# A fused mLSTM and expert layer on one core: the first chunk's exponents summed by TensorE, three steps moved from VectorE to ScalarE, and a new written order

## The chip, the cores and the metric

One core of a Trainium2 chip runs the whole program. The time of a run is the device time in microseconds (us) from start to end of the program; the span in a profile is the time from its first to its last instruction, and is a little shorter. The engines are TensorE (PE, matrix products into the accumulators in PSUM; PEld is its weight load), VectorE (DVE), ScalarE (ACT), GpSimd (POOL, which cannot read PSUM) and SyncE (SP, which issues the transfers).

## The reference

The first half is a recurrence with gates over 768 steps, for 4 batches and 8 heads of 40 numbers; the second half is an expert layer on its 3072 output rows.

```python
for t in range(S):
    m_new = maximum(f[t] + m, i[t])
    C = exp(f[t] + m - m_new) * C + exp(i[t] - m_new) * outer(v[t], k[t])
    n = exp(f[t] + m - m_new) * n + exp(i[t] - m_new) * k[t]
    y[t] = sigmoid(og[t]) * (C @ q[t]) / maximum(abs(n . q[t]), 1)
    m = m_new
h = x @ w_in                       # 320 -> 1024, x are the rows of y
solu = h * softmax(h)
out = (solu - mean) / sqrt(var + 1e-6) * g_ln @ w_out      # 1024 -> 320
```

The weights come as 64-bit floats, all else as 32-bit floats.

## The kernel before, in words

The sequence is cut into 6 chunks of 128 steps. A chunk of one batch is a unit; the 24 units run chunk by chunk, so units 0 to 3 are the first chunk of the four batches. In a unit the recurrence is done by matrix products: scores (`score`, L1186, keys by queries), times the decay matrix `d` (`p`, L1199), times the values (`intra`, L1253). From the second chunk on, the state `C` carried in is added (`inter`, L1226). All but the last chunk's units make a new state: `upd` (L1342) multiplies the weighted keys `kt` by the values into the one PSUM bank of the ring `so_`, and `add_c` brings it into `C` (L1369 adds; in the first chunk L1371 only copies, by VectorE, two copies of 64x164 a unit).

The decay matrix is exp(G[t] + b[s]) below the diagonal: G is the running sum of the log decays within a chunk (one row per head), and b = i - G - m is one number per step s and head. In chunks 1 to 5 a transfer spreads the rows of G over the partitions (`gb`), GpSimd masks it (L1102), and ScalarE takes the exponential with b as a bias per partition. Since a bias belongs to one head, this takes 8 ACTIVATEs of 128x128 a unit (`decay`, L1142). In the first chunk no transfer is used: `broad` (L1128) spreads G by 8 products a unit, each with one column of the identity as weights, into a PSUM tile of the ring `ph` (two tiles of 128x1024); the 8 exponentials read it there, and GpSimd masks the result.

A row of the unit's output is then divided (`rd`, L1269 and L1270; `sy` or `x`, L1274), gated (`x`), scaled by its largest number (`xm`, `xr`) and split into two 16-bit halves (`xq`, L1381 by ScalarE and L1388 by VectorE), turned by a transfer (`xT`), and multiplied with w_in (L1437, 16 products of 128x512 into `ph`, which is 128x1024). Row maximum (L1453), exponential (L1467), product (L1485), squares (L1495), a second split (`us`, L1546 and L1550), a second turning transfer into `big`, and 24 products with w_out (L1598) into `so_` follow.

Beside the first units the weights are prepared. `decode` turns a piece of 64-bit numbers into 32-bit ones: ScalarE scales the high words (`wt`, L677); for w_in it also scales the low words (`ls`, L686), and VectorE joins both (L694) and sets the sign (L738). For w_out (4 pieces of 128x640) VectorE shifts the high words (L711), brings in the low words itself (L727) and sets the sign (L738). w_in needs a scale known only when all six loads have landed (L793 to L849). w_out is later multiplied with a gain and a mean (L984), and split (L1000, L1008).

The order is written out by hand: `ORDER` is a list of operation numbers, of which a row may be a pair (two groups of products taken in turn) or may hold a number of keep-warm products to issue first (`fill`; L478, identity by identity, result unused). Each engine issues its own instructions in that order and waits in front of the first that isn't ready; so do the transfers on SP's queue.

## Time and profile before

| | |
|---|---|
| three runs | 298.85, 301.63 and 302.25 us, median 301.63 |
| the profiled execution | 300.66 us, of which 298.9 us are the span |
| busy in the span | PE 288.3 us, DVE 234.5, ACT 192.9, POOL 184.5 |
| mean granted TensorE clock | 0.989 of full speed |
| transfers | 56.13 MB, of which 35.69 MB are read from HBM |

A busy PE is not PE at its peak, since products are pipelined and their ends modelled. So the number that counts for PE here is the distance between the starts of two products, and whether another engine's instruction ended the wait before one.

### The profile page before, as it was taken

The numbers are of one execution on the slowest core, as the hardware profiler recorded it, in microseconds if no ns is written. First come the engines' busy times: TensorE is split into PE (matmuls) and PEld (weight loads), VectorE is DVE, ScalarE is ACT, GpSimd is POOL, SyncE is SP. The second block draws the span as 40 slices with busy tenths as digits, with TensorE's granted clock in tenths as the row PEclk, the third lists the DMA queues.
The fourth block names the chain that finished last, engine by engine and source line by source line (L and its number), as shares of the span: only waits on it lengthen the run. The fifth ranks groups of instructions, "written<-read, shape, count | busy, mean of one in ns | idle before, by whom it ended". The sixth has DMA issues, their size and how long they took to land.

```text
span 298.9 us, 6516 instructions
## 1 busy us (share of the span) xinstructions
PE 288.3 (96%) x2274; PEld 228.5 (76%) x2274; DVE 234.5 (78%) x605; ACT 192.9 (65%) x421; POOL 184.5 (62%) x241
## 2 busy tenths in 40 slices
PE   6789999989999999999999999999999999999995
PEld 6679997776588788786888888887787777756673
DVE  5788999977998887888878878977779878786221
ACT  2569569664587667858766857656766759565343
POOL 7047376960957795648963858649747453875321
PEclk9999999977999999999999999999999999999999
DMA  6979999375576685999969999788886981563811
GB/s 215 282 204 311 346 236 269 120 157 138 151 171 148 150 217 155 272 179 241 228 162 185 203 250 281 177 201 157 254 187 143 258 150 46 128 161 81 206 47 44
DMA packets 82640, 56.13 MB, mean 188 GB/s; under 512 B 66992, under 2 KB 73328, under 8 KB 82608
## 3 DMA queue, kind: packets, MB, share of 16 engines
q1 hardware_dynamic: 82608, 55.72, 76.4%
q8 instruction: 18, 0.29, 0.4%
q14 instruction: 14, 0.11, 0.1%
HBM read 35.69 MB, written 4.03 MB: 133 GB/s over the span
## 4 chain that ended last, share of the span: by engine, by line
PE 72%; DVE 15%; ACT 4%; DMA 3%; issue 3%; SPq 1%; POOL 0%; POOLq 0%; ACTq 0%; DVEq 0%
PE ph L1437 26%; PE sy L1253 8%; PE sy L1186 5%; PE sy L1226 4%; DMA big<-in_w_in_dram 3%; DVE p L1199 2%; DVE xq L1388 1%; DVE wg L738 1%; PE so__2413 L1598 1%; DVE wg L984 1%; PE so__999 L1598 1%; PE so__1676 L1598 1%; PE so__2597 L1598 1%; PE so__3057 L1598 1%; PE so__1227 L1598 1%
## 5 line engine op out<-in xcount | busy, mean ns | idle before, releaser
L1437 PE MATMUL ph<-wih,xT 128*128 128x512 f16 x240 | 76.1, 385 | 0.0
L1598 PEld LDWEIGHTS <-big 128*128 128x128 f16 x576 | 60.7, 110 | 19.6 <-issue 0.8
L1253 PEld LDWEIGHTS sy<-tk,p 128*128 128x128 f32 x384 | 59.8, 198 | 5.7 <-DVE sy L1239 1.1
L1437 PEld LDWEIGHTS <-xT 128*128 128x128 f16 x384 | 46.1, 122 | 21.7 <-issue 2.2
L1142 ACT ACTIVATE d<-gb,bG 128x128 f32<-128x128 f32 x160 | 49.9, 390 | 19.6 <-POOL gb L1102 7.1
L1253 PE MATMUL sy<-tk,p 128*128 128x41 f32 x384 | 57.8, 253 | 0.7 <-DVE sy L1239 0.7
L1550 POOL TENSOR_TENSOR us<-e,us 128x1024 f16<-128x1024 f32 x23 | 49.0, 2130 | 9.6 <-ACT us L1546 9.4
L1437 PE MATMUL ph<-wil,xT 128*128 128x512 f16 x144 | 49.2, 387 | 0.0
L1467 ACT ACTIVATE e<-ph,nh,hs 128x1024 f32<-128x1024 f32 x24 | 28.8, 1198 | 21.0 <-DVE nh L1460 15.5
L1453 DVE TENSOR_REDUCE nm<-ph 128x1 f32<-128x1024 f32 x24 | 29.2, 1216 | 7.7 <-PE ph L1437 7.6
L1199 DVE TENSOR_TENSOR p<-sy,d 128x512 f32<-128x512 f32 x48 | 32.3, 681 | 2.4 <-PE sy L1186 2.2
L1485 DVE SCALAR_TENSOR_TENSOR e<-ph,s,e 128x1024 f32<-128x1024 f32 x24 | 30.7, 1277 | 2.5 <-ACT e L1467 2.0
L1226 PEld LDWEIGHTS sy<-C,qk 128*128 128x128 f32 x160 | 26.9, 191 | 3.2 <-PE ph L1437 0.7
L1495 ACT ACTIVATE sq<-e,a 128x1024 bf16<-128x1024 f32 x24 | 27.4, 1140 | 2.1 <-DVE e L1485 2.1
L1546 ACT CAST us<-e 128x1024 f16<-128x1024 f32 x23 | 23.8, 1036 | 7.3 <-DVE e L1485 7.3
L1186 PE MATMUL sy<-qk 40*128 40x128 f32 x384 | 27.9, 285 | 0.0
L1580 POOL TENSOR_TENSOR pw<-ab,mhalf 128x1 f32<-128x1 f32 x24 | 14.2, 592 | 21.4 <-DVE ab L1574 21.2
L1186 PEld LDWEIGHTS sy<-qk 40*128 40x128 f32 x384 | 23.3, 187 | 4.0 <-issue 2.5
L1226 PE MATMUL sy<-C,qk 128*128 128x82 f32 x160 | 26.0, 258 | 0.2 <-DVE p L1199 0.2
L1304 POOL TENSOR_TENSOR x<-x,sg 128x320 f32<-128x320 f32 x20 | 17.3, 865 | 14.2 <-DVE x L1274 13.9
L1102 POOL TENSOR_SCALAR_AFFINE_SELECT gb<-gb 128x1024 f32<-128x1024 f32 x20 | 22.5, 1125 | 5.1 <-DMA gb<-gd 4.9
L1168 POOL TENSOR_TENSOR kt<-tk,d 128x320 f32<-128x320 f32 x20 | 16.4, 820 | 12.2 <-PE so__3024 L1342 3.2
(257 smaller groups left out, 572.7 us busy)
## 6 DMA issues: line engine op xcount, KB each, us to landing
gb<-gd SPq DMA_DIRECT2D x20, 512.0 KB
tk<-in_tok_dram SPq DMA_DIRECT2D x24, 324.0 KB
qk<-in_qkT_dram SPq DMA_DIRECT2D x48, 160.0 KB
sg<-in_og_dram SPq DMA_DIRECT2D x12, 320.0 KB
out_dram<-ot SPq DMA_DIRECT2D x24, 160.0 KB
big<-in_w_out_dram SPq DMA_DIRECT2D x4, 640.0 KB
big<-in_w_in_dram SPq DMA_DIRECT2D x4, 512.0 KB
big<-in_w_in_dram SPq DMA_DIRECT2D x2, 256.0 KB
```

The source lines that it names most:

```text
L1142: nc.scalar.activation(out=P[d_t][:, j, n, :], in_=exponent(P, h), func=AF.Exp, bias=P[BG][:, 0, c, b * H + h : b * H + h + 1],)
L1186: nc.tensor.matmul(P[ps[j]][:, n * L : (n + 1) * L], lhsT=P[qk][r, 1, n, :], rhs=P[qk][r, 0, n, :], start=True, stop=True,)
L1199: lambda P, j=j: V.tensor_tensor(out=P[p_t][:, j], in0=P[ps[j]].rearrange("p (n l) -> p n l", l=L), in1=P[d_t][:, j], op=ALU.mult,),
L1226: nc.tensor.matmul(P[yk][:, n * 2 * E1 : (n + 1) * 2 * E1], lhsT=P[qk][:, 0, n, :], rhs=P[old][:, n, :], start=first_of_bank(), stop=False ...
L1253: nc.tensor.matmul(yv(P)[:, h, :], lhsT=P[p_t][:, j, n, :], rhs=v1(P)[:, h, :], start=first_of_bank(), stop=True, skip_group_check=True,)
L1437: nc.tensor.matmul(P[ph][:, j * 512 : (j + 1) * 512], lhsT=P[xT][:, a, :], rhs=P[w][:, k, j * 512 : (j + 1) * 512], start=n == 0, stop=n == 7,
L1453: lambda P: V.tensor_reduce(out=P[nm], in_=P[ph], axis=AX.X, op=ALU.max, negate=True),
L1467: lambda P: nc.scalar.activation(out=P[e], in_=P[ph], func=AF.Exp, bias=P[nh], scale=P[hs], accum_out=P[z]),
L1485: lambda P: V.scalar_tensor_tensor(out=P[e], in0=P[ph], scalar=P[s2], in1=P[e], op0=ALU.mult, op1=ALU.mult, accum_out=P[a]),
L1495: lambda P: nc.scalar.activation(out=P[sq], in_=P[e], func=AF.Square, bias=P[a], scale=-float(DFF), accum_out=P[su]),
L1550: lambda P: nc.gpsimd.tensor_tensor(out=P[us][:, 1], in0=P[e], in1=P[us][:, 0], op=ALU.subtract),
L1598: nc.tensor.matmul(P[po][:, 0:DM], lhsT=uTv(P, a)[:, k, :], rhs=P[w][:, k, :], start=n == 0, stop=n == 23)
```

## The change

1. In the first chunk `broad` issues a second product per head: the weights are b (laid out in a second 128 columns of the tile `e`, the rest of which is zero), the moving operand is one column of the identity, repeated. It adds b[s] to G[t] in PSUM. The exponent is then whole, and `decay` is one ACTIVATE of 128x512 for each of the two halves of a unit, in place of four of 128x128. b for these units is made by two subtractions of 32x128 on VectorE (`mk_b0`), and GpSimd sets the columns to zero first.
2. The state copies of the first chunk go to ScalarE (`nc.scalar.copy`).
3. `W_OUT_ACT` is True: the low words of w_out are scaled by ScalarE, as those of w_in were, and VectorE joins the words in one instruction in place of two.
4. Keep-warm products may also be issued after the first-layer tiles are in use, into the PSUM tile that the next group of products will overwrite.
5. `ORDER` is new. It holds 17 keep-warm products where there were 55; one more stands outside it in both.

```diff
 RANK = {
+    "act cn": (0.76, 0.0, 0.0),
...
 ORDER = [
-    8, 3, 6, 146, 5, 0, 30, 28, 1, 32, 11, 34, 4, 27, 36, 9, 25, 38, 286, 26, 24, (18, -1, 5), 10, 7, 127, 47, 2, 192,
+    8, 5, 11, 6, 12, 7, 32, 34, 0, 36, 38, 1, 4, 9, 26, 40, 3, 2, 29, 129, 288, 27, (20, -1, 3), 10, 49, 128, 13, 130,
...
+            late = self.first[self.fill[2][1]] in issued
+            for _ in range(0 if late else filled.get(n, 0)):
                 self.fill[1](self)
...
+            for _ in range(filled.get(n, 0) if late else 0):
+                self.fill[3](self, self.tiles[new[0]])
...
+    B0 = (*G_, 1)
+    P.op(POOL, 210, lambda P: nc.gpsimd.memset(P[G_][:, S : S + L], 0.0), [B0], prio=-84, lock=False)
...
+    def mk_b0(P):
+        o = P[G_][0 : B * H, S : S + L]
+        V.tensor_tensor(out=o, in0=gt(P, I_)[:, 0:L], in1=gt(P, G_)[:, 0:L], op=ALU.subtract)
+        V.tensor_tensor(out=o, in0=o, in1=gt(P, M_)[:, 0:L], op=ALU.subtract)
...
-    W_IN_ACT, W_OUT_ACT = True, False
+    W_IN_ACT, W_OUT_ACT = True, True
...
                         rhs=P[G_][:, 0:L],
                         start=True,
+                        stop=False,
+                    )
+                    nc.tensor.matmul(
+                        exponent(P, h),
+                        lhsT=P[G_][:, S : S + L],
+                        rhs=P[I][:, r : r + 1].to_broadcast([L, L]),
+                        start=False,
                         stop=True,
                     )
...
         def decay(P, j):
             begun_in.add((*d_t, j))
+            if c == 0:
+                nc.scalar.activation(
+                    out=P[d_t][:, j],
+                    in_=P[src].rearrange("p (i two l) -> p two i l", two=2, l=L)[:, j],
+                    func=AF.Exp,
+                )
+                return
...
-                    V.tensor_copy(out=P[cn][r, :, w], in_=o)
+                    nc.scalar.copy(out=P[cn][r, :, w], in_=o)
```

Three places of the new order follow. The first is TensorE while the first units' decay is made, from the last product of the w_in scale (L837, in the change L855) on. Before, units 0 and 1 have had their spreading products by then, and the list goes on so (`so__267` is unit 0's new state, `qk_112` and `qk_103` hold the queries and keys of units 0 and 1):

```order
L837 MATMUL so__215<-wa_219,ones 128x1
L1186 MATMUL sy<-qk_112 128x128 x8
L478 MATMUL so__215<-ident 128x128
L1342 MATMUL so__267<-tk,kt_97 128x82 x4
L1253 MATMUL sy<-tk,p 128x41 x4
L1128 MATMUL ph<-e,ident 128x128 x8
L1253 MATMUL sy<-tk,p 128x41 x4
L1186 MATMUL sy<-qk_103 128x128 x8
```

In the change (of 32 exponent products of units 1 and 2, which stand in turn, the first two are shown, and of unit 3's 16 none):

```order
L1218 MATMUL sy<-qk_99 128x128 x8
L855 MATMUL so__201<-wa_215,ones 128x1
L1146 MATMUL ph<-e,ident 128x128
L1153 MATMUL ph<-ident,e 128x128
...
L1285 MATMUL sy<-tk,p 128x41 x8
L1218 MATMUL sy<-qk_115 128x128 x8
...
L1374 MATMUL so__450<-tk,kt_108 128x82 x4
L486 MATMUL ph<-ident 128x128 x3
```

Unit 0's products with the values (L1253, now L1285) and its state product (L1342, now L1374) now stand behind the exponents of units 1 and 2, and the state product behind those of unit 3 too.

The second place is VectorE, where unit 0's second 16-bit half has been made (before, the first row here; in the change it stands seven rows ahead) and w_out's pieces are decoded among the first units. Before:

```order
L1388 SCALAR_TENSOR_TENSOR xq<-x,xr,xq 128x64
L711 TENSOR_SCALAR wg<-wt 128x640 x2
L738 SCALAR_TENSOR_TENSOR wf<-big,wf 128x512
L727 SCALAR_TENSOR_TENSOR wg<-big,wg 128x640 x2
L738 SCALAR_TENSOR_TENSOR wg<-big,wg 128x640
L1313 TENSOR_REDUCE xm<-x 128x1
L1314 TENSOR_SCALAR xm<-xm 128x1
L1315 RECIPROCAL xr<-xm 128x1
L1371 COPY C_262<-so__466 64x4x41
```

In the change:

```order
L1231 TENSOR_TENSOR p<-sy,d 128x512 x2
L712 SCALAR_TENSOR_TENSOR wg<-wt,ls 128x640
L756 SCALAR_TENSOR_TENSOR wg<-big,wg 128x640
L1301 RECIPROCAL rd<-sy 128x8
L1302 SCALAR_TENSOR_TENSOR rd<-rd 128x8
L1345 TENSOR_REDUCE xm<-x 128x1
```

The shift and the separate low-word step are one instruction now (L712), and the state copies are gone from this engine.

The third place is ScalarE in the same stretch. Before:

```order
L1142 ACTIVATE d<-ph,bG 128x128 x8
L1381 ACTIVATE xq<-x,xr 128x320
L1142 ACTIVATE d<-ph,bG 128x128 x4
L677 ACTIVATE wt<-big 128x640 x2
L1090 ACTIVATE sg<-sg 128x640
L1142 ACTIVATE d<-gb,bG 128x128 x4
```

In the change (`C_320` and `C_403` are the new states of units 0 and 1):

```order
L1166 ACTIVATE d<-ph 128x512 x3
L887 CAST wih<-wf 128x512
L695 ACTIVATE wt<-big 128x640
L704 ACTIVATE ls<-big 128x640
L1403 COPY C_320<-so__450 64x4x41
L1166 ACTIVATE d<-ph 128x512
L704 ACTIVATE ls<-big 128x640
L1174 ACTIVATE d<-gb,bG 128x128 x4
L1403 COPY C_320<-so__450 64x4x41
L695 ACTIVATE wt<-big 128x640
L704 ACTIVATE ls<-big 128x640
L1403 COPY C_403<-so__528 64x4x41
```

The state copies and the low words stand among the exponentials; the second copy of a state stands behind exponentials of unit 4 (`d<-gb`).

On SP's queue the first write of G to the scratch in HBM (`gd`, L563, now L581), which waits for the running sum, stood ahead of the first loads of tokens (`tk`) and gates (`sg`); now three loads of each stand ahead of it.

More of the change, by code (lines that the diff above doesn't have):

```diff
@@ L384, in run @@
         skip = set(joint.values())
+        self.needs()
+        issued = set()
         for n in order:
@@ L390, in run @@
                 out = out + ops[joint[n]][3]
-            for _ in range(filled.get(n, 0)):
+            late = self.first[self.fill[2][1]] in issued
+            for _ in range(0 if late else filled.get(n, 0)):
                 self.fill[1](self)
-            for k in out:
-                if k[:2] not in self.tiles:
-                    self.tiles[k[:2]] = self.tags[k[0]][1]()
+            new = [k[:2] for k in out if k[:2] not in self.tiles]
+            for k in new:
+                self.tiles[k] = self.tags[k[0]][1]()
+            for _ in range(filled.get(n, 0) if late else 0):
+                self.fill[3](self, self.tiles[new[0]])
+            issued.update((n, joint.get(n, n)))
             if n in joint:
@@ L559, in mlstm_moe_kernel @@
     )
+    def mk_b0(P):
+        o = P[G_][0 : B * H, S : S + L]
+        V.tensor_tensor(out=o, in0=gt(P, I_)[:, 0:L], in1=gt(P, G_)[:, 0:L], op=ALU.subtract)
+        V.tensor_tensor(out=o, in0=o, in1=gt(P, M_)[:, 0:L], op=ALU.subtract)
+    P.op(DVE, 440, mk_b0, [B0], [I_, G_, M_], prio=g0, lock=True)
     for b in range(B):
@@ L1132, in broad @@
                         start=True,
+                        stop=False,
[5 more added lines that the diff above has]
+                        start=False,
                         stop=True,
                     )
-            op(PE, 1900, broad, [src], [I, G_], name="g")
+            op(PE, 3700, broad, [src], [I, G_, B0], name="g")
         def decay(P, j):
             begun_in.add((*d_t, j))
+            if c == 0:
[5 more added lines that the diff above has]
+                return
             for n in range(NP):
@@ L1149, in unit @@
         for j in range(2):
-            op(ACT, 1560, lambda P, j=j: decay(P, j), [(*d_t, j)], [src, (*BG, 0)])
+            op(ACT, 660 if c == 0 else 1560, lambda P, j=j: decay(P, j), [(*d_t, j)], [src] if c == 0 else [src, (*BG, 0)])
         if c == 0:
@@ L1370, in add_c @@
                 else:
-                    V.tensor_copy(out=P[cn][r, :, w], in_=o)
+                    nc.scalar.copy(out=P[cn][r, :, w], in_=o)
             for j in range(2):
-                op(DVE, 322, lambda P, j=j: add_c(P, j), [(*cn, j)], [pu], name="cn")
+                op(DVE if c > 0 else ACT, 322 if c > 0 else 360, lambda P, j=j: add_c(P, j), [(*cn, j)], [pu], name="cn")
             Ccur[b] = cn
@@ L1632, in mlstm_moe_kernel, with idle_in @@
         unit(u)
-    P.fill = (216, idle, (("so_", "idle"), ("ph", "wm")))
+    def idle_in(P, t):
+        nc.tensor.matmul(t[:, 0:L], lhsT=P[I], rhs=P[I], start=True, stop=True)
+    P.fill = (216, idle, (("so_", "idle"), ("ph", "wm")), idle_in)
     with tc.manual_schedule():
```

120 rows, old and new, of the table ORDER are left out of this document.

## The prediction

> **What bounds the kernel now.** I read the page's busy shares and its chain first, then a table of windows cut where the chain changes engine, then the chain in order of time. From the page (busy us of each engine; the chain that ended last, by engine):
>
> ```profile
> PE 288.3 (96%) x2274; PEld 228.5 (76%) x2274; DVE 234.5 (78%) x605; ACT 192.9 (65%) x421; POOL 184.5 (62%) x241
> PE 72%; DVE 15%; ACT 4%; DMA 3%; issue 3%; SPq 1%; POOL 0%; POOLq 0%; ACTq 0%; DVEq 0%
> ```
>
> PE leads, but 15% of the chain is VectorE's. The windows (busy us and instructions of PE, PEld, DVE, ACT and POOL, then clock, transfer share and GB/s) say where:
>
> ```profile
> 0.00:18.00 18.00, 12.98 (x99) 11.69 (x101) 11.07 (x22) 6.21 (x16) 7.46 (x23) 1.00 0.87 249
> 18.00:28.00 10.00, 9.79 (x95) 9.18 (x92) 9.04 (x24) 9.82 (x23) 5.77 (x5) 1.00 0.74 254
> 28.00:38.00 10.00, 10.00 (x103) 9.66 (x101) 9.87 (x18) 6.50 (x17) 4.41 (x4) 1.00 0.95 326
> 38.00:48.00 10.00, 10.00 (x92) 9.43 (x92) 9.80 (x22) 7.11 (x19) 6.47 (x5) 1.00 1.00 264
> 48.00:63.40 15.40, 13.74 (x102) 10.69 (x100) 14.95 (x39) 10.57 (x25) 11.88 (x14) 1.00 0.68 182
> 63.40:71.00 7.60, 7.60 (x32) 5.57 (x32) 4.64 (x13) 4.68 (x14) 4.48 (x4) 0.55 0.70 104
> 71.00:82.00 11.00, 10.54 (x85) 7.31 (x83) 10.40 (x19) 5.97 (x13) 6.85 (x5) 1.00 0.53 144
> 82.00:180.00 98.00, 97.96 (x792) 78.29 (x793) 81.78 (x229) 70.12 (x153) 67.83 (x88) 1.00 0.90 197
> ```
>
> From 18 to 63.4 us VectorE is busy 43.66 of 45.4 us. PE looks as full, but part of that is keep-warm products. From 82 us on, PE is busy for 97.96 of 98 us while VectorE has a sixth to spare. The chain agrees (start, us, what):
>
> ```profile
> 4.26 10.27 DMA big<-in_w_in_dram
> ...
> 28.56 3.07 DVE wf L694 x2
> ...
> 63.71 3.56 PE sy L1253 x16
> ...
> 72.38 2.86 DVE wg L984 x6
> ...
> 82.04 1.11 PE so__999 L1598 x7
> ```
>
> So there are three stages. Up to about 18 us the w_in loads and the scale made from them lead. Up to 82.04 us, when the first product with w_out starts, VectorE leads with the units and the weights, except where TensorE ran at 0.55 of its clock (63.4 to 71 us). Then PE leads to the end. Only the second stage is cut by what the change takes off VectorE.
>
> **VectorE's part.** What leaves it, and the nearest thing to what stays:
>
> ```profile
> 19.33 1.28 DVE L694 SCALAR_TENSOR_TENSOR wf<-wt,ls 128x512 int32<-128x512 int32 x2
> 20.53 0.68 DVE L738 SCALAR_TENSOR_TENSOR wf<-big,wf 128x512 int32<-128x512 int32 x1
> 21.73 0.65 DVE L1371 COPY C<-so__267 64x164 f32<-64x164 f32 x2
> 36.21 0.89 DVE L711 TENSOR_SCALAR wg<-wt 128x640 int32<-128x640 int32 x2
> 37.01 0.69 DVE L738 SCALAR_TENSOR_TENSOR wf<-big,wf 128x512 int32<-128x512 int32 x1
> 37.62 1.55 DVE L727 SCALAR_TENSOR_TENSOR wg<-big,wg 128x640 int32<-128x640 int32 x2
> ```
>
> Two state copies take 0.65 us, so eight take 2.6. Two shifts (L711) hold the engine from 36.21 to the next start at 37.01, 0.40 each, so four are 1.6. The joining instruction that replaces L727 is of L694's form: 1.20 us from start to start for two of 512 columns is 0.75 for one of 640, against 0.78 for L727: nothing. That is 4.2 us off an engine that has no other gap to fill. `mk_b0`'s two small subtractions fall at about 9 to 10 us, ahead of the w_in loads' end at 14.5, and cost nothing while these loads lead; without that cover they would cost less than one of the copies above.
>
> **ScalarE's part.** It takes these on, and must not become late. Its rows:
>
> ```profile
> 11.16 0.36 ACT L604 ACTIVATE bG<-bG 128x192 f32<-128x192 f32 x1 [3.18 <-DVE bG L597]
> 25.79 2.16 ACT L1142 ACTIVATE d<-ph,bG 128x128 f32<-128x128 f32 x8
> 39.29 0.80 ACT L677 ACTIVATE wt<-big 128x640 f32<-128x640 f32 x1
> 288.88 0.58 ACT L1530 CAST big<-ph 128x512 f16<-128x512 f32 x1
> ```
>
> Eight copies, bounded by the 128x192 row at 0.36, are 2.9 us; four low-word steps at 0.80 are 3.2. The exponentials shrink: 32 at 2.16/8 = 0.27 are 8.6 us, and eight of 128x512 out of PSUM, nearest to the 0.58 us cast out of the same kind of tile, are 4.6. Net 2.1 us more. ScalarE is idle for 11.4 of the 45.4 us between 18 and 63.4, so I count nothing; without that cover it is the 2.1.
>
> **TensorE's part.** Its rows:
>
> ```profile
> 17.15 0.38 PE L837 MATMUL so__215<-wa,ones 1*128 1x1 f32 x2
> ...
> 20.92 2.03 PE L1128 MATMUL ph<-e,ident 128*128 128x128 f32 x16
> 22.79 0.98 PE L1253 MATMUL sy<-tk,p 128*128 128x41 f32 x8
> ...
> 28.36 1.88 PE L1253 MATMUL sy<-tk,p 128*128 128x41 f32 x16
> 30.17 1.16 PE L1186 MATMUL sy<-qk 40*128 40x128 f32 x16
> 31.26 3.39 PE L478 MATMUL ph<-ident 128*128 128x128 f32 x28
> 38.30 4.49 PE L478 MATMUL ph<-ident 128*128 128x128 f32 x38
> ```
>
> A 32-bit product is two instructions. 14 keep-warm products take 3.39 us (0.24 each); from start to start, 8 spreading products take 1.87 (0.234 each), 8 value products 1.81, 8 scores 1.09. Up to the first product with w_out, the change has 38 keep-warm products fewer (-9.1 us), 32 exponent products more (+7.5), and one unit's scores fewer (-1.1, which come back after it): -2.7 us. PE is not what leads there, so this only shows that the exponents find room where keep-warm products stood.
>
> Their place does cost something. Behind L837 (done at 17.5 us) the new order puts the 32 exponent products of units 1 and 2, to 25.0, and then unit 0's value products, to 26.8; before, their second half began at 22.79 and was done at 23.8. VectorE has ten instructions of 0.60 us and three small ones (0.7) to do from about 18.1: it runs dry at 24.8 and waits 2.0 us for unit 0. In the window from 18 to 28 it was idle for 0.96 before. So +1.0. The later products wait behind them on PE, scores of unit 1 first.
>
> Unit 0's own exponents are complete later too (they wait for `mk_b0`), near 14 us; exponentials and GpSimd's mask follow to about 16.3, still ahead of the 18.1 us at which the scale releases VectorE: nothing, as long as the loads land as before.
>
> **After 82 us.** One unit's scores come back (+1.1), and 22 more products stand in pairs with first-layer ones, of which six are value products. The rows of such pairs:
>
> ```profile
> 45.14 0.39 PE L1437 MATMUL ph<-wih,xT 128*128 128x512 f16 x1
> 45.37 0.31 PE L1253 MATMUL sy<-tk,p 128*128 128x41 f32 x2
> 45.51 0.39 PE L1437 MATMUL ph<-wih,xT 128*128 128x512 f16 x1
> ```
>
> A value product in a pair costs the 0.14 us from 45.37 to 45.51, against 1.81/8 = 0.23 alone; if all 22 saved that much, -2.0; I take half, -1.0, and the two terms cancel.
>
> **SP's queue.** Three loads each of `tk` and `sg` no longer wait behind the first write of G. The w_in loads stay ahead of them on the queue, so I count nothing for the loads that lead; if they shared the transfer engines instead, one pair of these,
>
> ```profile
> tk<-in_tok_dram SPq DMA_DIRECT2D x24, 324.0 KB
> sg<-in_og_dram SPq DMA_DIRECT2D x12, 320.0 KB
> ```
>
> at the 249 GB/s of the first window, would delay the scale by 2.6 us.
>
> **The sum.** 300.66 (the profiled execution; its span is 298.9, and 1.76 lie around it) - 4.2 + 1.0 = 297.5 us. That execution is 0.97 below the median of the three runs, 301.63, and inside their spread of 298.85 to 302.25, so I let 297.5 stand as the forecast of the median too.
>
> **The half-clock stretch.** The sum keeps it as it was. The row of 63.4 to 71 us prices it: 7.6 us at 0.55 of the clock lose 0.45 x 7.6 = 3.4 us of PE's work. Before it stands this wait:
>
> ```profile
> 61.81 0.27 PE L942 MATMUL ph<-ident,wmx 128*1 128x128 f32 x1 [0.80 <-DMA gb<-gd]
> ```
>
> The longest gap there is 0.80 us. The Trainium skill (TensorE: Matmul & The Clock Gate, section "Why this matters for your kernels") asks only that no gap between bursts exceeds about 3 us. By that rule this stretch should not be there, so the trace disagrees: short gaps among narrow 32-bit products were enough.
>
> **The rivals.**
>
> First, the forecast: VectorE's stage is shorter by 3.2 us; 297.5; chance 0.50.
>
> Second, PE stays warm all through: no gap of a window's length arises and the stretch at 63.4 goes. That takes 3.4 us more off: 294.1. Against it is the stretch that a gap of 0.80 us brought. Chance 0.08.
>
> The rule of the Trainium skill cited above (TensorE: Matmul & The Clock Gate, section "Why this matters for your kernels") would make this second case the likely one.
>
> Third, VectorE's gain isn't used: PE, which lost only 2.7 us of work before 82 us, becomes what leads, as the 2.0 us wait for unit 0 already hints; then the gain is at most 2.7 less the 1.0, so 299.0. For it: PE was busy 43.5 of the 45.4 us to 63.4. Against: the two keep-warm rows above alone, 33 products, are 7.9 us of that. Chance 0.19.
>
> Fourth, one more half-clock stretch, since 38 keep-warm products are gone, and of the 33 of the two rows above only 5 are left in their stretch of the order: 297.5 + 3.4 = 300.9. For it, the short gaps that were enough; against it, that the exponent products are as wide as those they replace. Chance 0.13.
>
> Fifth, slower: the state copies on ScalarE hold the one `so_` bank. The second copy of each state stands behind unit 4's or later exponentials, which in turn wait on another engine; the next unit's state product (L1374) waits for that bank, and all of PE's queue behind it. Such a wait of ScalarE was, before,
>
> ```profile
> 44.23 2.45 ACT L1142 ACTIVATE d<-gb,bG 128x128 f32<-128x128 f32 x8 [2.24 <-DVE p L1199]
> ```
>
> 2.24 us; four units of it are 9.0, so 297.5 + 9.0 = 306.5. It decides from the point at which a copy starts later than PE reaches the next state product. Against it: by the counts above unit 0's state product is near 35 us and the next one some 5 us later. Chance 0.10.
>
> **How the numbers follow.** About 1%, 3 us, is what a measurement of this kernel can tell from no change: faster means below 298.6, slower above 304.6. The forecast with its own bounds (0 to -4.2 on VectorE's gain, 0 to 2.6 for the loads, -1.0 to 1.1 after 82 us) lies mostly below 298.6: I give 0.44 of its 0.50 to faster and 0.06 to within 1%. With the second case faster is 0.52; the third and fourth make within 1% 0.38; slower is 0.10. The range goes from the second case, 294.1, to the fourth, 300.9, which leaves out the fifth and the tails.
>
> **What would show it.** Right: the first product with w_out starts near 79 us and not at 82; VectorE's busy time from 18 to 63.4 us stays above 95% but its work ends earlier; ScalarE's copies don't end a wait of PE; from then on PE is busy without gaps for the same 217 us. Wrong: the first w_out product starts no earlier (third), the granted clock shows a second stretch below full speed (fourth), or PE's L1374 waits on ScalarE's L1403 (fifth). What would make the whole sum wrong is a gap in the PE stage after 82 us, which I count at nothing because the order there is made of the same steps.

## The result, and the profile after

The changed kernel takes 304.16 us (median of 20 runs, 300.99 to 308.06), the kernel before 301.79 us (20 runs beside them). The ratio is 1.0125, 95% interval 1.0092 to 1.0159: slower by about 1%. The ratios here and below leave out executions over 1.5% above the fastest of their kernel, so they are not the quotients of the medians (1.0079 here). The prediction was 297.5 us, 294.1 to 300.9, and faster. The profiled execution took 304.69 us, of which 302.7 are the span, against 300.66 and 298.9.

The page of the changed kernel, busy time of each engine and the chain of waits by engine:

```profile
PE 288.5 (95%) x2262; PEld 230.2 (76%) x2262; DVE 232.8 (77%) x595; ACT 192.9 (64%) x409; POOL 180.7 (60%) x242
PE 79%; DVE 12%; DMA 4%; ACT 2%; issue 1%; SPq 1%; ACTq 0%; DVEq 0%
```

The same windows as in the prediction (start and end, length, busy us and instructions of PE, PEld, DVE, ACT and POOL, clock, transfer share, GB/s):

```profile
0.00:18.00 18.00, 14.01 (x79) 13.14 (x79) 10.12 (x16) 2.52 (x4) 3.93 (x17) 1.00 0.89 240
18.00:28.00 10.00, 10.00 (x96) 9.74 (x94) 8.24 (x21) 9.25 (x17) 5.77 (x8) 1.00 0.83 252
28.00:38.00 10.00, 10.00 (x100) 9.54 (x99) 9.07 (x20) 7.61 (x15) 7.10 (x9) 1.00 0.73 204
38.00:48.00 10.00, 9.28 (x86) 7.97 (x86) 9.83 (x20) 8.00 (x20) 6.73 (x7) 1.00 0.75 220
48.00:63.40 15.40, 13.55 (x92) 10.79 (x94) 14.08 (x36) 9.81 (x25) 5.98 (x8) 1.00 0.86 194
63.40:71.00 7.60, 7.60 (x64) 6.29 (x63) 7.26 (x20) 6.36 (x20) 5.64 (x6) 1.00 0.86 234
71.00:82.00 11.00, 8.33 (x63) 6.50 (x62) 10.67 (x22) 7.03 (x14) 7.54 (x6) 0.93 0.79 229
82.00:180.00 98.00, 96.31 (x783) 76.80 (x782) 79.44 (x209) 67.41 (x153) 67.98 (x90) 0.99 0.88 189
```

Three things differ. VectorE no longer fills its stage: from 18 to 63.4 us it is busy for 41.22 of 45.4 us, where it was 43.66. The half-clock stretch of 63.4 to 71 us is gone, but there is a piece of one in the row of 71 to 82 us. And in the last row TensorE is idle for 1.69 us, where it was idle for 0.04.

The rows of TensorE (start, us, what; behind it the idle time before it and what ended that) show where the time went:

```profile
6.78 4.21 PE L486 MATMUL so__93<-ident 128*128 128x128 f32 x18
...
13.05 0.64 PE L1153 MATMUL ph<-ident,e 128*128 128x128 f32 x2
13.48 0.63 PE L1146 MATMUL ph<-e,ident 128*128 128x128 f32 x2
...
19.22 0.38 PE L855 MATMUL so__201<-wa,ones 1*128 1x1 f32 x2
...
80.00 1.60 PE L1258 MATMUL sy<-C,qk 128*128 128x82 f32 x8 [2.51 <-DVE x L1306]
81.39 0.47 PE L1630 MATMUL so__972<-woh,big 128*128 128x320 f16 x1
...
129.07 0.42 PE L1285 MATMUL sy<-tk,p 128*128 128x41 f32 x2 [1.53 <-DVE sy L1271]
```

Nine keep-warm products take 4.21 us (2.27 before), and the first exponent products stand 0.43 us apart, against 0.225 later on. The last product of the w_in scale starts at 19.22 us, not 17.15, though the loads had landed. The first product with w_out starts at 81.39 us, hardly ahead of 82.04, and just before it TensorE waits 2.51 us, at 80.00. From there to the end it is 302.7 - 81.39 = 221.3 us, against 298.9 - 82.04 = 216.9. So of the 3.8 us lost, the part ahead of that product gives -0.65 and the part behind it +4.4. Forecast were -3.2 and 0.

The chain of waits between the two stages has a piece that the kernel before has not. From 44 to 62 us it runs through ScalarE, SP's queue and a transfer of `sg`:

```profile
49.23 0.68 SPq L1449
...
52.19 7.90 DMA sg<-in_og_dram
...
60.75 0.82 ACT wj L771 x2
```

What this piece costs is not separated: TensorE is idle for 1.85 us from 48 to 63.4 us, and was for 1.66 before.

### The profile page after: what moved, and what is told of

Read it like the earlier page. It is cut to its first block, busy times and chain, and to the rows that moved or that the text cites. A ratio compares the mean times of both kernels' runs of the same rounds, so it can differ in the third digit from the quotient of the medians.

```text
span 302.7 us, 6478 instructions
## 1 busy us (share of the span) xinstructions
PE 288.5 (95%) x2262; PEld 230.2 (76%) x2262; DVE 232.8 (77%) x595; ACT 192.9 (64%) x409; POOL 180.7 (60%) x242
## 4 chain that ended last, share of the span: by engine, by line
PE 79%; DVE 12%; DMA 4%; ACT 2%; issue 1%; SPq 1%; ACTq 0%; DVEq 0%
PE ph L1469 23%; PE sy L1285 9%; PE sy L1218 7%; PE sy L1258 4%; PE sy L1630 3%; DVE xq L1420 3%; DMA sg<-in_og_dram 3%; PE ph L1146 2%; PE ph L1153 2%; DVE wg L1002 2%; DVE p L1231 1%; PE so__972 L1630 1%; PE so__93 L486 1%; DVE nm L1485 1%; PE so__3471 L1630 1%
## 5 line engine op out<-in xcount | busy, mean ns | idle before, releaser
L1469 PE MATMUL ph<-wih,xT 128*128 128x512 f16 x240 | 79.3, 381 | 0.0
L1630 PEld LDWEIGHTS <-big 128*128 128x128 f16 x576 | 61.4, 112 | 20.1
L1285 PEld LDWEIGHTS sy<-tk,p 128*128 128x128 f32 x384 | 58.1, 192 | 7.6 <-DVE sy L1271 2.3
L1285 PE MATMUL sy<-tk,p 128*128 128x41 f32 x384 | 56.2, 247 | 2.4 <-DVE sy L1271 1.7
L1469 PE MATMUL ph<-wil,xT 128*128 128x512 f16 x144 | 47.7, 380 | 0.0
L1258 PEld LDWEIGHTS sy<-C,qk 128*128 128x128 f32 x160 | 28.4, 194 | 7.3 <-issue 4.8
L1258 PE MATMUL sy<-C,qk 128*128 128x82 f32 x160 | 27.6, 262 | 3.8 <-DVE x L1306 2.5
L1218 PE MATMUL sy<-qk 40*128 40x128 f32 x384 | 28.8, 285 | 0.4 <-DVE xm L1345 0.3
L1420 DVE SCALAR_TENSOR_TENSOR xq<-x,xr,xq 128x256 f16<-128x256 f32 (+1 forms) x48 | 26.5, 592 | 0.3 <-ACT xq L1413 0.3
L1200 POOL TENSOR_TENSOR kt<-tk,d 128x320 f32<-128x320 f32 x20 | 14.9, 745 | 12.6 <-PE so__2929 L1374 2.4
```

The lines of the kernel that those rows point to most:

```text
L1218: nc.tensor.matmul(P[ps[j]][:, n * L : (n + 1) * L], lhsT=P[qk][r, 1, n, :], rhs=P[qk][r, 0, n, :], start=True, stop=True,)
L1258: nc.tensor.matmul(P[yk][:, n * 2 * E1 : (n + 1) * 2 * E1], lhsT=P[qk][:, 0, n, :], rhs=P[old][:, n, :], start=first_of_bank(), stop=False ...
L1285: nc.tensor.matmul(yv(P)[:, h, :], lhsT=P[p_t][:, j, n, :], rhs=v1(P)[:, h, :], start=first_of_bank(), stop=True, skip_group_check=True,)
L1420: V.scalar_tensor_tensor(out=P[xq][:, o : o + w], in0=P[x][:, n : n + w], scalar=P[xr], in1=P[xq][:, n : n + w], op0=ALU.mult, op1=ALU.sub ...
L1469: nc.tensor.matmul(P[ph][:, j * 512 : (j + 1) * 512], lhsT=P[xT][:, a, :], rhs=P[w][:, k, j * 512 : (j + 1) * 512], start=n == 0, stop=n == 7,
L1630: nc.tensor.matmul(P[po][:, 0:DM], lhsT=uTv(P, a)[:, k, :], rhs=P[w][:, k, :], start=n == 0, stop=n == 23)
```

## The experiments

Each ratio is to the kernel before on the same chip, with its 95% interval. The granted clock of a kernel differs from one execution to the next (for the kernel before between 0.983 and 0.999 in most), and the time with it: on the chip of k1 to k4 the kernel before took 298.7 us on average in nine executions at 0.994 and 301.5 us in five at 0.989. So the spans of single profiles are compared only with their clocks beside them. The columns after the ratio come from the profiled execution: span and clock, the start of the last product of the w_in scale, the start of the first product with w_out, and what remains from there. Three rows have no such columns: their traces (310.45, 303.40 and 306.45 us) are of executions well above the medians of their kernels (304.70, 297.99 and 302.21 us). Nor is any other trace the median one: that of m1 is the second slowest of twelve executions, that of k3 the quickest of twelve (299.27 us, median 302.20).

| kernel | ratio | span, clock | scale | first w_out | rest |
|---|---|---|---|---|---|
| before | 1 | 298.9, 0.989 | 17.15 | 82.04 | 216.9 |
| changed | 1.0125 [1.0092, 1.0159] | 302.7, 0.994 | 19.22 | 81.39 | 221.3 |
| e1_new_code_old_order | 1.0132 [1.0073, 1.0192] | 301.5, 0.998 | 20.27 | 84.17 | 217.3 |
| e2_old_code_new_order | 1.0407 [1.0340, 1.0473] | 309.3, 0.955 | 18.06 | 87.9 | 221.4 |
| e3_warm_start | 1.0128 [1.0052, 1.0204] | | | | |
| f1_exponents_only | 1.0218 [1.0169, 1.0268] | 301.3, 0.998 | 20.27 | 84.43 | 216.9 |
| m2_exponents_units_0_1 | 1.0122 [1.0043, 1.0201] | 300.9, 0.994 | 20.58 | 83.99 | 216.9 |
| k4_exponents_units_2_3 | 1.0049 [1.0001, 1.0097] | 301.0, 0.994 | 18.71 | 84.06 | 216.9 |
| f3_scale_first | 1.0254 [1.0212, 1.0296] | 305.8, 0.989 | 17.88 | 88.27 | 217.5 |
| f2_new_order_no_exponents | 1.0067 [1.0039, 1.0094] | 298.9, 0.988 | 17.32 | 76.70 | 222.2 |
| k1_copies_only | 0.9893 [0.9830, 0.9956] | 295.1, 1.000 | 17.75 | 78.17 | 216.9 |
| k2_low_words_only | 0.9961 [0.9907, 1.0015] | 296.6, 0.994 | 17.36 | 79.45 | 217.2 |
| e5_offload_only | 0.9954 [0.9911, 0.9996] | | | | |
| m1_offload_again | 0.9920 [0.9873, 0.9966] | 298.2, 0.994 | 18.65 | 80.58 | 217.6 |
| h4_before_no_fill | 1.0125 [1.0043, 1.0207] | 302.2, 0.955 | 17.39 | 85.33 | 216.9 |
| h2_offload_no_fill | 1.0105 [1.0051, 1.0159] | 300.8, 0.959 | 17.50 | 83.16 | 217.6 |
| h1_new_code_no_fill | 1.0227 [1.0150, 1.0305] | 302.4, 0.977 | 19.95 | 85.46 | 216.9 |
| f4_new_front_old_rest | 1.0195 [1.0154, 1.0237] | 302.2, 0.988 | 18.51 | 83.65 | 218.5 |
| h3_new_front_no_exponents_old_rest | 1.0089 [1.0039, 1.0138] | | | | |
| k3_w_out_before_inter | 1.0077 [1.0031, 1.0122] | 297.3, 1.000 | 17.04 | 75.95 | 221.4 |

The last column reads itself: with the old order the rest is 216.9 to 217.6 us in twelve kernels, whatever came before; with the new order it is 221.3 to 222.2 in four.

### Order or code?

The new code in the old order, with the two new steps put in:

```diff
 ORDER = [
-    8, 5, 11, 6, 12, 7, 32, 34, 0, 36, 38, 1, 4, 9, 26, 40, 3, 2, 29, 129, 288, 27, (20, -1, 3), 10, 49, 128, 13, 130,
+    8, 3, 6, 148, 5, 0, 32, 30, 1, 34, 11, 12, 36, 4, 29, 38, 9, 27, 40, 288, 28, 26, (20, -1, 5), 10, 7, 129, 49, 2,
+    194, 13, 14, 55, 33, (19, -1, 9), 16, 128, 37, 130, 132, 21, 35, 22, 31, 39, 178, 134, 41, 177, 133, 23, 42, 43,
...
```

> All three code changes (exponents summed by TensorE, state copies and low words of w_out on ScalarE), but the old written order, with two rows added for the two new small steps. If the loss lies in the new order (cold start and late scale, then gaps after 82 us), this is not slower than before: VectorE's 4.2 us less against about 2 us of scale that now waits behind 32 exponent products, so about 0.7 to 1.0% faster, near 299 us. If the loss lies in the exponent products themselves, it is as slow as the changed kernel, 1.01 to 1.02 of before.

And the old code in the new order, the same exchange the other way (without the two new steps):

> The old code (exponents with a bias in four ACTIVATEs, copies and low words on VectorE) in the new written order with its 17 keep-warm products; four rows stand later since their inputs come later. If the order is what costs, it is the slowest: the changed kernel's +1.25% and the 4.2 us of VectorE's work back, 1.02 to 1.03 of before. If the code is what costs, about 1.00.

The new code costs 1.3% in the old order too, so the new order is not needed for the loss. The old code in the new order is 4% slower, with clocks of 0.940 to 0.955 in all six executions, so that order suits the old code still less. Which of the two carries the changed kernel's loss these runs don't say; a table further down does.

The third idea was the cold and late start. The identity and the i gates were put first, and the first group of keep-warm products made longer:

```diff
-    8, 5, 11, 6, 12, 7, 32, 34, 0, 36, 38, 1, 4, 9, 26, 40, 3, 2, 29, 129, 288, 27, (20, -1, 3),
+    8, 0, 6, 5, 11, 12, 7, 32, 34, 36, 38, 1, 4, 9, 26, 40, 3, 2, 29, 129, 288, 27, (20, -1, 5),
```

> The changed kernel with the start of before alone put back: the identity made first on GpSimd, the i gates loaded ahead of the f gates, and two more keep-warm products ahead of the first transposes. If the cold start is what costs, the scale of w_in is released 2 us earlier (18.0 instead of 20.1 us in the profile) and the time is 2 us below the changed kernel, 0.993 of it, that is 1.005 to 1.007 of before. If the loss is made after 82 us, the 2 us are lost in a wait later on and the time stays at 1.012 of before.

Its ratio is 1.0128, but the interval of 1.0052 to 1.0204 holds both expectations: the run does not decide what the start costs.

### The exponents

Only the exponents, in the kernel before and in its order; then in units 0 and 1 alone, and in units 2 and 3 alone (the condition shown is that of the last):

```diff
+        V.tensor_tensor(out=o, in0=gt(P, I_)[:, 0:L], in1=gt(P, G_)[:, 0:L], op=ALU.subtract)
...
+                        stop=u < 2,
+                    )
+                    if u < 2:
+                        continue
+                    nc.tensor.matmul(
```

> The kernel before in its own order, with only the exponents changed (mk_b0, two products per head, two ACTIVATEs a unit); state copies and w_out's low words stay on VectorE. Theory A: the 16 more products of units 0 and 1 hold the scale of w_in (in the old order both units stand ahead of its transpose), about 2 us, and the later ones cost a little: ratio to before 1.010 to 1.020. Theory B: the exponents were free, and the loss of the new code in the old order comes from the three parts together: 0.998 to 1.005.

> The kernel before in its own order with the whole exponents in units 0 and 1 alone, the 16 products that stand ahead of the scale of w_in (3.75 us of TensorE). All four units cost 2.18%, units 2 and 3 alone 0.49%. If products ahead of the scale of w_in cost more than later ones, 1.013 to 1.020, and the scale is done some 2 us later than in the kernel before. If the two halves cost the same and the whole is more than their sum, 1.004 to 1.009.

> The kernel before in its own order with the whole exponents in units 2 and 3 alone (16 more products, 3.75 us of TensorE); units 0 and 1, whose products stand ahead of the scale of w_in, stay as before. All four units alike cost 2.18%. If the products cost as work on TensorE's queue wherever they stand, half of that: 1.008 to 1.013. If the cost came from holding the scale of w_in, 1.000 to 1.005.

All four units cost 2.18%, 6.5 us: nearly all of the 7.5 us that their products take. The two halves are 1.22% and 0.49%; together 1.7%, and the intervals of each are wide. The chain of waits of the kernel with all four (start, us, what) shows why. From 18.60 to 59 us it runs through TensorE's queue, but for one step of VectorE of 0.29 us, and the keep-warm products, unchanged, stand in it:

```profile
18.60 0.33 PE sy L632 x2
...
20.34 0.31 PE so__232 L855 x2
...
36.94 1.09 PE sy L1218 x16
38.03 3.32 PE ph L486 x28
41.35 0.85 PE so__485 L1374 x8
...
45.17 4.32 PE ph L486 x38
```

The scale of w_in is the first that is late: its last product starts at 20.27 us, behind 32 exponent products, where it starts at 17.15 to 18.71 without them in units 0 and 1. So I moved unit 1's products behind the scale, in the new code and the old order:

```diff
-    194, 13, 14, 55, 33, (19, -1, 9), 16, 128, 37, 130, 132, 21, 35, 22, 31, 39, 178, 134, 41, 177, 133, 23, 42, 43,
-    176, 44, 180, 15, 135, 24, 222, (45, -1, 3), 137, 46, 136,
+    194, 13, 14, 55, 33, (19, -1, 9), 16, 128, 37, 130, 132, 21, 35, 22, 31, 39, 134, 41, 177, 133, 23, 42, 43,
+    176, 44, 15, 135, 24, 222, (45, -1, 3), 178, 180, 137, 46, 136,
```

> The new code in the old order, with unit 1's 16 exponent products moved behind the two TensorE steps of the w_in scale. Theory A (they hold the scale): most of the 1.3% comes back, 1.000 to 1.004, and the first product with w_out starts near 82 us where it started at 84.2. Theory B (the exponents cost wherever they stand, as work of TensorE): 1.010 to 1.014.

This was a miss for both theories: slower still, 1.0254. The scale came in time (17.88 us), but now unit 0's scores stood behind those products. VectorE's row in that kernel, and its window from 18 to 28 us:

```profile
23.22 0.69 DVE L1231 TENSOR_TENSOR p<-sy,d 128x512 f32<-128x512 f32 x1 [3.77 <-PE sy L1218]
```

```profile
18.00:28.00 10.00, 9.90 (x91) 9.48 (x92) 5.80 (x13) 5.22 (x10) 3.45 (x4) 1.00 0.34 100
```

It waits 3.77 us, and is busy for 5.80 of 10. So it is not the scale as such: TensorE's queue is full there, and whatever stands behind the added 3.7 us comes late.

In the new order the exponents were taken out, and the copies and low words left on ScalarE:

```diff
-                        stop=False,
-                    )
-                    nc.tensor.matmul(
-                        exponent(P, h),
-                        lhsT=P[G_][:, S : S + L],
-                        rhs=P[I][:, r : r + 1].to_broadcast([L, L]),
-                        start=False,
                         stop=True,
...
-            if c == 0:
-                nc.scalar.activation(
```

> The changed kernel in its new order, but the first chunk's exponents as before (8 products and 8 ACTIVATEs with a bias a unit); copies and low words on ScalarE. If the exponent products are what costs in the new order too, it is faster than the changed kernel by 1 to 2%: ratio to before 0.995 to 1.003. If the new order needs ScalarE's shorter exponentials, it is slower than the changed kernel, 1.02 to 1.04, near the 1.04 of the old code in the new order.

1.0067, between the two expectations. The first product with w_out started at 76.70 us, 4.7 us earlier than in the changed kernel, at a lower clock; the rest was as long as with the exponents (222.2). So they seem to cost here too, by about 0.6%, less than in the old order; the two intervals just touch.

(In this kernel, and in f4, h3 and k3 below, the list also has two early entries of different engines, 6 and 11, exchanged. In the traces of this kernel and of k3 no engine's own order differs by that.)

Four kernels have the state copies and the low words on ScalarE, and differ in order and exponents alone:

| ratio to before | old order | new order |
|---|---|---|
| without the exponents | 0.9954 and 0.9920 (e5, m1) | 1.0067 (f2) |
| with the exponents | 1.0132 (e1) | 1.0125 (changed) |

Without the exponents the new order costs 1.1 to 1.5%; in the old order the exponents cost 1.8 to 2.1%. Either alone loses more than the steps on ScalarE gain, and the second on top of the first adds 0.6% or nothing. What the new order gains ahead of the first w_out product (76.70 us in f2, 80.58 in m1) it loses behind it (222.2 against 217.6).

### The keep-warm products

My forecast took them for room. The 14 and 19 in front of the first-layer tiles were removed in three kernels: before, before with the offloads, and new code in the old order.

```diff
-(239, -1, 14)
+239
...
-(285, -1, 19)
+285
```

> The kernel before less the same 33 keep-warm products and nothing else: a control. If VectorE led its stage up to 82 us, as the chain of waits has it, and the clock holds: 0.995 to 1.003. If TensorE led: 0.975 to 0.985. If these products held the clock up: 1.008 to 1.025.

> The kernel before in its own order with the state copies and w_out's low words on ScalarE (0.9954), less the same 33 keep-warm products. Theory A (TensorE's queue led there with these products on it, so VectorE's 4.2 us could not show): 0.980 to 0.990. Theory B (they cover waits and hold the clock): 0.995 to 1.010.

> The new code in the old order (1.0132 with its 55 keep-warm products), less the 14 and 19 keep-warm products in front of the first-layer tiles of the first units. Theory A: in that order TensorE's queue leads up to 59 us (its chain of waits holds 3.32 and 4.32 us of just these products), so 7.6 us less on it let the exponents' 7.5 in: ratio to before 0.992 to 1.004. Theory B: these products cover waits for VectorE and keep the clock up; without them the time stays or a half-clock stretch of 3.4 us comes: 1.010 to 1.025.

None was faster without them, and two were slower clear of noise: 1.0125 against 1 and 1.0105 against 0.9920 to 0.9954. In the third, 1.0227 against 1.0132, the intervals overlap. The kernel before shows what they did. TensorE's row behind the removed products, and its windows:

```profile
33.95 1.97 PE L1342 MATMUL so__451<-tk,kt 128*128 128x82 f32 x8 [2.38 <-DVE C L1371]
```

```profile
30.00:32.00 2.00, 1.57 (x21) 1.33 (x20) 2.00 (x3) 0.85 (x3) 2.00 (x2) 1.00 1.02 406
32.00:34.00 2.00, 0.05 (x1) 0.08 (x1) 1.90 (x5) 1.37 (x2) 0.46 (x1) 0.75 0.95 368
34.00:36.00 2.00, 2.00 (x10) 2.00 (x10) 1.97 (x5) 0.34 (x2) 0.00 (x0) 0.50 1.01 244
...
44.00:48.00 4.00, 4.00 (x20) 3.94 (x20) 4.00 (x10) 3.52 (x11) 0.51 (x1) 0.50 1.04 342
48.00:52.00 4.00, 4.00 (x26) 3.31 (x24) 1.04 (x3) 2.64 (x5) 4.00 (x4) 0.50 1.09 296
52.00:56.00 4.00, 4.00 (x12) 1.98 (x11) 3.47 (x11) 1.69 (x5) 3.85 (x5) 0.50 0.18 35
56.00:60.00 4.00, 4.00 (x35) 2.96 (x33) 1.22 (x4) 2.02 (x5) 2.24 (x4) 0.89 0.45 152
```

Where they stood is now one wait of 2.38 us for VectorE, and behind it the clock is at half until about 57 us, 23 us on, though TensorE is busy without a gap from 44 to 56 us (a second wait, of 1.46 us, ends at 42.89). It is no accident of one execution: all six of this kernel have a clock of 0.966 or less. By the rule that the prediction cites (Trainium skill, TensorE: Matmul & The Clock Gate, section "Why this matters for your kernels": no gap over about 3 us between bursts) a gap of 2.38 us should do no harm; the trace disagrees again. A gap is not even needed: in f3 the half clock begins at 71.02 us, and the longest gap in the 9 us before it is 0.16 us.

The clock is not the only thing that differs. The chain of waits of this kernel goes through GpSimd where VectorE led before, up to 42.89 us (pieces of "issue", in which the profile shows no wait, are left out):

```profile
24.55 2.25 POOL wil L877 x2
...
31.30 1.17 POOL kt L1168
...
42.11 0.74 POOL kt L1168
...
42.89 2.00 PE so__534 L1342 x8
```

The other two have GpSimd there too. How much of the loss is the clock and how much GpSimd is not separated. So these products stand in the chain when TensorE leads (f1), but taking them out saved time in none of the three.

### VectorE's steps

Copies alone, low words alone, and both, in the kernel before and its order:

```diff
-                    V.tensor_copy(out=P[cn][r, :, w], in_=o)
+                    nc.scalar.copy(out=P[cn][r, :, w], in_=o)
```

```diff
-    W_IN_ACT, W_OUT_ACT = True, False
+    W_IN_ACT, W_OUT_ACT = True, True
```

> The kernel before in its own order with the first chunk's eight state copies on ScalarE and nothing else (2.6 us off VectorE by the prediction). If VectorE leads its stage, 0.989 to 0.993. If TensorE's queue leads it, 0.997 to 1.001. If the copies hold the one bank of the new states, above 1.003.

> The kernel before in its own order with w_out's low words on ScalarE and nothing else (1.6 us off VectorE by the prediction). If VectorE leads its stage, 0.993 to 0.996. If TensorE's queue leads, or ScalarE pays for it, 0.998 to 1.004.

> The kernel before, in its own order, with the state copies and the low words of w_out on ScalarE, and no exponent products. If VectorE's stage to 82 us sets the time, as the prediction had it, 4.2 us less on VectorE give about 0.986 to 0.99 of before. If what leaves VectorE there is not on the path, 1.00. If the copies on ScalarE hold the state bank, over 1.00 with waits of TensorE on ScalarE's copies.

> State copies and w_out's low words on ScalarE in the old order, once more, on another chip and with a profile at full clock. Alone the copies gave 0.9893 and the low words 0.9961, together 0.9954 the first time. If the two gains add (VectorE leads, the first measurement was at the edge of its interval), 0.984 to 0.990. If ScalarE, with 6 us more of its own, or TensorE's queue takes the lead, 0.993 to 0.999 again, and the chain of waits from 18 to 60 us is ScalarE's or TensorE's and not VectorE's.

The copies give 0.9893: 3.2 us, where I had 2.6. The low words give 0.9961, 1.2 us (I had 1.6), with 1 inside the interval. Both together give 0.9954 and 0.9920, less than the copies alone, though the intervals overlap. Part of the 3.2 us is the clock's: at 0.998 or more the copies alone took 296.3 us (two executions) against 298.8 of the kernel before (three), and at 0.994 297.7 (two) against 298.7 (nine). At 0.994 the low words alone took 298.6 us (four), no less than the kernel before, and both together 298.3 (three) and 298.6 (five) on their chips. So the copies are worth some 1 to 2.5 us, nothing is shown of the low words, and that both together gain less than the copies is not shown either.

Two reasons why more need not help are in the traces. With the copies gone TensorE's queue leads from 16 to 53 us. The chain of the kernel with the copies alone:

```profile
31.93 3.32 PE ph L479 x28
...
39.07 4.32 PE ph L479 x38
...
52.03 1.14 PE sy L1187 x16
53.35 0.48 issue
53.83 2.38 DVE wg L739 x2
```

In the kernel before these places of the chain were VectorE's (28.56 to 60 us). By this chain, what more is taken off VectorE there doesn't shorten it. And the low words on ScalarE make VectorE wait. Its waits with the low words alone, from 18 to 82 us:

```profile
DVE wg L694 <- ACT ls L686: 1.3, 2, 1.0
```

Two waits in this trace, 1.3 us beside the 1.6 that I had counted as saved.

### The new order's rest, and the wait at 80 us

The new order up to unit 0's first group with w_out (step 170) and the old sequence behind it, with the exponents and without:

```diff
-    123, 170, 163, 620, 208, 426, 171, 522, 571, 240, 127, 294, 480, 209, 478, 295, 252, 524, 210, 172, (482, 296),
...
+    123, 389, 426, 524, 525, 526, 571, 477, 163, 621, 478, 522, 528, 620, 170, 480, 127, (171, 481), 208, 172, 173,
+    168, 210, (482, 294), 240, 169, 252, 385, 211, 174, 295, 253, 175, 483, 254, 286, (388, 296), 255, 573, 484, 212,
...
```

> The new code, in the new order up to unit 0's first group of products with w_out and in the old order's sequence behind it. The changed kernel took 221.3 us from that product to its end, the kernel before 216.9. If the rest of the new order is what costs there, the ratio to before is 0.997 to 1.003. If it is what the front leaves behind (units further on or back, a cold clock), it stays at 1.010 or above.

> The changed kernel without the whole exponents, in the new order up to unit 0's first group of products with w_out (it started at 76.70 us there) and in the old order's sequence behind it (216.9 us in the kernel before). If the two parts add, the span is 294 to 295 us and the ratio to before 0.983 to 0.990. If the old sequence only moves the work ahead of that product, as with the exponents in (83.65 us in place of 81.39), it is 1.000 to 1.010.

Both failed to add up. With the exponents the rest fell from 221.3 to 218.5 us, of which about 1.2 are a stretch at half clock, but the first w_out product came 2.3 us later, and the ratio rose to 1.0195. Without them it is 1.0089, no better than 1.0067. Half of one order does not fit half of the other.

Last, the wait of 2.51 us. VectorE and GpSimd ahead of it, in the changed kernel:

```profile
77.39 1.35 DVE L1302 SCALAR_TENSOR_TENSOR rd<-rd 128x8 f32<-128x8 f32 x1
...
79.36 0.49 DVE L1306 SCALAR_TENSOR_TENSOR x<-rd,sy 128x320 f32<-128x320 f32 x1
```

```profile
74.29 4.44 POOL L1026 TENSOR_TENSOR wol<-wg,woh 128x640 f16<-128x640 f32 x3 [4.04 <-ACT woh L1018]
78.69 0.73 POOL L1200 TENSOR_TENSOR kt<-tk,d 128x320 f32<-128x320 f32 x1
```

`rd` on 8 numbers takes 1.35 us, until GpSimd's row ends at 78.73; at 110.40 it takes 0.17. (The kernel before has such a row too, 1.13 us at 77.67.) The products with the carried state wait for the `x` behind it. I moved them behind the first two steps with w_out:

```diff
-    118, 344, 114, 125, 345, 204, 119, 721, 476, 623, 518, 126, 572, 251, 434, 115, 342, 205, 435, 206, 341, 479, 207,
-    123, 170, 163, 620, 208, 426, 171, 522, 571, 240, 127, 294, 480, 209, 478, 295, 252, 524, 210, 172, (482, 296),
+    118, 344, 114, 125, 345, 204, 119, 721, 476, 623, 518, 126, 572, 251, 434, 115, 342, 205, 435, 206, 341, 207, 123,
+    170, 163, 208, 426, 171, 479, 620, 522, 571, 240, 127, 294, 480, 209, 478, 295, 252, 524, 210, 172, (482, 296),
```

> The changed kernel with one row of its order moved: the products with the carried state that made TensorE wait 2.51 us for VectorE at 80.00 us now stand behind the first two steps of products with w_out. GpSimd has the low halves these need ready at 78.73 us. If this wait is part of what the changed kernel lost, its ratio to before falls from 1.0125 by 0.4 to 0.8%, to 1.004 to 1.009. If TensorE only waits later, it stays at 1.010 to 1.015.

1.0077, in the range of the first expectation; its interval still overlaps that of 1.0125, so a gain is not shown. TensorE now waits in front of the w_out products, for less:

```profile
75.95 0.30 PE L1630 MATMUL so__966<-woh,big 128*128 128x320 f16 x1 [1.61 <-DVE mx L1508]
```

This execution ran at full clock from 9 us on, and its rest is 221.4 us, of which the eight products moved behind the first w_out product take 0.85. That is still 3.6 us more than the kernel before: what the new order loses there is not mainly the clock.

A version that beats both kernels came out: the kernel before with only the state copies moved, 297.73 us against 301.32 in the medians (0.9893 [0.9830, 0.9956]; about 1 to 2.5 us at equal clock).

## Why the prediction was wrong

**VectorE's part** (-4.2 us) was not reached: both steps together give 1.4 and 2.4 us in two measurements of the old order. The copies alone agree with the 2.6 (3.2 measured, 1 to 2.5 at equal clock); for the low words no gain is shown. I had read the stage as VectorE's alone. But in the chain of the kernel before ScalarE has the stretch from 18.80 to 28 us, with rows such as this one,

```profile
25.91 2.05 ACT d L1142 x8
```

and once VectorE's copies were gone, TensorE's queue led.

**TensorE's part** is the step that failed first. "The exponents find room where keep-warm products stood" put 38 x 0.24 us of those against 7.5 us of exponents. That term was nothing in the sum, and the exponents alone measured 6.5 us (f1, 2.2%, all keep-warm products left in). In the old order there is no such room: a keep-warm product is an instruction of the queue like any other. Left in, it stands in the chain ahead of what comes behind it (f1); taken out, the clock falls and nothing is gained (h4: 1.2% slower). In the new order the exponents cost about 0.6%. And the new order's keep-warm products were not cheap in this trace: its 18 take 2.07 + 4.21 + 0.87 + 0.65 = 7.80 us, 0.43 each, since 13 of them ran at half pace. The third rival, TensorE leads and the gain is unused, had this mechanism, and I argued against it with just these products ("33 products, are 7.9 us of that"). Its 299.0 us still had TensorE's work fall by 2.7 us, and so its time was too low.

**Unit 0's exponents and the scale of w_in** ("nothing, as long as the loads land as before"): the loads landed, but the scale's first product stood behind exponents at half pace. The rows of VectorE in the changed kernel, and the first of them in k3, which has the same order up to there and ran at full pace from 9 us on:

```profile
18.23 0.28 DVE L845 TENSOR_REDUCE wa<-so__201 1x1 f32<-1x128 f32 x1 [2.54 <-PE so__201 L842]
...
28.69 0.21 DVE L1301 RECIPROCAL rd<-sy 128x8 f32<-128x8 f32 x1 [1.45 <-PE sy L1285]
```

```profile
16.06 0.28 DVE L845 TENSOR_REDUCE wa<-so__201 1x1 f32<-1x128 f32 x1 [0.45 <-PE so__201 L842]
```

2.5 us where I had 0, but 0.45 in k3, as much as in the kernel before: the 2.5 belong to the slow start of this execution, and at full pace the step was right. The second row is the **+1.0**: a wait of 1.45 us for unit 0's values, forecast 2.0 (1.46 in k3). That the scale itself sets the time is not shown; f3 speaks against it.

**ScalarE's part** was right in its sizes (eight exponentials of 128x512 take 0.60 us each, forecast 0.58; a copy 0.29, bound 0.36), and no copy ended a wait of TensorE: the fifth rival is out. But in the old order its low words made VectorE wait 1.3 us (k2).

**The half-clock stretch** did not stay: it went from 63.4 us and a shorter one came at 80.0 to 83.6 us, behind the 2.51 us wait, at 0.56 of the clock. It is not a fixed part of the kernel before either: its executions at 0.994 are 2.9 us quicker than those at 0.989 (chip of k1 to k4); the profile that the sum began from is one with the longer stretch.

**After 82 us** (0) is the largest miss: +4.4. Adding up the distances from start to start of TensorE's products behind the first w_out product in both traces gives its parts. The one unit's scores are 1.6 us, where I had 1.1. Idle time adds 1.75 us, of which 1.69 are at 116.92 and 129.07. The products with w_out take 1.35 us more, since 2.6 us of them ran at half clock. The value, state and inter products, which stand more often in pairs, take only 0.4 us less, where I had 1.0 for the pairs. So the idle time and the clock, which I had put at nothing, make 3.1 of the 4.4 us; the two terms that were to cancel leave 1.2. The longer idle time has this before it (f2 and k3 have the same wait of 1.53 us):

```profile
122.61 3.41 DVE L1420 SCALAR_TENSOR_TENSOR xq<-x,xr,xq 128x256 f16<-128x256 f32 x2
```

```profile
122.58 2.13 POOL L1582 TENSOR_TENSOR us<-e,us 128x1024 f16<-128x1024 f32 x1 [1.45 <-ACT us L1578]
124.66 1.29 POOL L1120 TENSOR_SCALAR_AFFINE_SELECT gb<-gb 128x1024 f32<-128x1024 f32 x1
```

The split that takes 0.68 us in the kernel before (at 113.02) takes 3.41 beside GpSimd: it ends 0.07 us after GpSimd's second row does. That agrees with a rule of the Trainium skill (SBUF — State Buffer, section "SBUF: two separate sides"): VectorE with two inputs from SBUF and GpSimd lock one pair of ports against each other for a whole instruction. I had looked for gaps only in whether "the order there is made of the same steps", and not at which steps of VectorE the new order sets beside GpSimd. No run took this meeting apart, so its price is read from the trace only.

Of the signs named: the first product with w_out came at 81.39 us and not near 79, VectorE was busy for 91% of 18 to 63.4 us and not 95%, and the gap behind 82 us, which I had said would make the whole sum wrong, is there.

What stays open: why the two halves of the orders don't combine, why exponents and order cost less together than one by one, and how much of the 1.25% is the wait at 80 us, the exponents (about 0.6%) and the rest (4.4 us in the trace); these overlap, and the runs don't split them cleanly.

## What to carry to other kernels

Work that fills a queue to keep a clock up is not slack: it can stand in the chain ahead of other work, and without it the clock may fall. So before counting on its room, see what the chain becomes when the first leader is shortened; engines within a few us of each other share the lead (here VectorE, ScalarE, TensorE and GpSimd each had it in one kernel or another). Compare executions at equal clock before a gain of 1% is put down to a change. And where an order written by hand changes, the steady part behind the place under study is a term of its own: compare its length in both profiles before the front's.

## What the runs showed of the hardware

Behind a gap of 2.38 us TensorE ran at half its clock for some 23 us, 12 of them (44 to 56 us) without any idle time; in f3 a stretch of 6.8 us at half clock began with no gap over 0.16 us in the 9 us before. In the clock records that the traces keep, the stretches at half clock that end before the kernel does last 3.41, 6.83, 10.24, 13.65, 20.48 or 23.90 us, whole multiples of 3.41. One instruction on 128x8 numbers took 1.35 us beside GpSimd, and a pair of 128x256 and 128x64 took 3.41 in place of 0.68. Two executions of nearly the same program start at different paces: the first exponent products stand 0.43 us apart in the changed kernel, and 0.225 in the one with a single row moved. These early paces don't show in the clock column: it reads 1.00 for the first 18 us of both.
